# Moving the low-part subtractions of a split-precision attention and MoE kernel from GpSimd to VectorE

## Chip, cores and metric

The kernel runs on one core of a Trainium2 chip. The metric is the device time of one execution in microseconds (us). PE is TensorE, DVE is VectorE, ACT is ScalarE, POOL is GpSimd, SP is SyncE.

## Reference

```python
scores = scale * np.matmul(q, k.transpose(0, 1, 3, 2))   # 4 x 8 heads, 768 positions, 64 wide
keep = is_sink | in_window                               # 4 sink columns, a window of 128
a = softmax(np.where(keep, scores, -1e9))
x = np.matmul(a, v).transpose(0, 2, 1, 3).reshape(B * S, H * D)   # 3072 x 512
a = x @ w_a          # 512 x 1536
b = x @ w_b          # 512 x 1536
return (a * b @ w_out).astype(np.float32)                # 1536 x 512
```

The three weight matrices come as 64-bit floats; everything else is 32-bit.

## The kernel before

**Two halves.** A number that must be multiplied more exactly than one TensorE pass allows is kept as a high part (rounded to the type `F32R`) and a low part (the number less its high part). A product is then three matmuls: high by high, low by high, high by low. So every weight tile and every intermediate tile `g` (`a * b` of the MoE) needs a low part, which is one subtraction of 128x512 (`g` of the first chunk and all weights) or 128x384 and 128x256 (`g` of later chunks).

**Chunks.** The 3072 rows are worked through in 8 chunks (`CHUNKS`). The attention of chunk 0 (4 blocks of 128 rows) stands alone; then the MoE of chunk c (function `moe`) runs while the attention of chunk c + 1 is fed into it in small steps (`between`). The MoE goes over 12 values of j (`NJ`). For each j: `half("a", j)` (L686, 12 matmuls of up to 512 columns), ACT copies `a` out (L705), `half("b", j)` (L686), DVE multiplies the two into `g` (L711), ACT rounds `g` to `gh` (L714), one engine makes the low part `gl` (L716), and PE adds the product of the j before to the outputs (`project`, L695). `g` has one buffer, `gh` and `gl` two each.

**Attention of chunk 1.** It belongs to the MoE of chunk 0: a unit is a score matmul (L548) into the PSUM tile `s`, of which there is one; DVE reads it (L555), ACT takes the exponential (L557), DVE two small steps (L559, L560), ACT scales (L564), POOL copies 8 sink columns (L569), PE transposes (L585), ACT copies (L586), PE multiplies by v (L602), ACT copies the result (L604). So the next L548 waits until L555 has read the last one.

**Weights.** They are made once, 36 tiles of 128x512 in the order a, b, o of j = 0, 1, ..., from step 18 of the first attention on and throughout the MoE of chunk 0. The function `weights_to` sends each tile k through three stages, and a step does the low part of tile k - 4, the high part of tile k - 3 and the bits of tile k: `weight_low` (L317: subtraction), `weight_high` (L312: ACT rounds), `weight_bits` (L301 and L303 on DVE, L302 on ACT, L305 on POOL: the addition of the low words, 128x512). Before the change the low parts of the b tiles are made on POOL and those of the a and o tiles on DVE. `gl` is made on POOL for j below 10 and on DVE for j = 10 and 11, in every chunk.

**Order.** A scheduler puts each engine's instructions in order when the kernel is built; instructions passed through `keep_in_program_order` (`pin`) stay among themselves in the order in which they were written. Each engine runs its own list strictly in that order. By the order written, the low part of tile b of j + 1 stands behind L303 of tile b of j + 2 and in front of L301 of tile o of j + 2.

Of the kernel before, what the change touches and what calls it, by code (L numbers as in the profile page):

```python
# [7 lines left out]
F32 = mybir.dt.float32  # L8
# [5 lines left out]
ALU = mybir.AluOpType  # L14
# [3 lines left out]
B, H, S, D = 4, 8, 768, 64  # L18
DM, FF = 512, 1536
P = 128  # L20
# [3 lines left out]
NJ = FF // P  # L24
# [6 lines left out]
NEG = 8.0e9  # L31
BIG = 3.0e38
NIO = 6
POOL_LOW = (1, 3)
STEP0, STEPS = 18, 3
AHEAD, LOADS = 3, 9
D1, D2 = 3, 4
# [181 lines left out]
class Fast:  # L219
# [70 lines left out]
        self.nc.sync.dma_start(raw, self.src(kind)[j].bitcast(I32))  # L290
        self.raw[kind, j] = raw

    def low_engine(self, kind, j):
        return self.nc.gpsimd if (3 * j + "abo".index(kind)) % POOL_LOW[1] == POOL_LOW[0] else self.nc.vector

    def weight_bits(self, kind, j):
        nc, pin = self.nc, self.tc.keep_in_program_order
        rv = self.raw[kind, j].rearrange("p (n c) -> p n c", c=2)
        lo, hi = rv[:, :, 0], rv[:, :, 1]
        f = self.io([P, DM], I32, f"wf_{kind}{j}")  # L300
        pin(nc.vector.tensor_scalar(f, hi, 3, 0x3FFFFFF8, op0=ALU.logical_shift_left, op1=ALU.bitwise_and))  # L301
        pin(nc.scalar.activation(lo, lo.bitcast(U32), AF.Copy, scale=2.0 ** -29))  # L302
        nc.vector.scalar_tensor_tensor(out=f, in0=hi, scalar=I_TOP2, in1=f,  # L303
                                       op0=ALU.bitwise_and, op1=ALU.bitwise_or)
        nc.gpsimd.tensor_tensor(f, f, lo, op=ALU.add)  # L305
        del self.raw[kind, j]
        self.wf[kind, j] = f.bitcast(F32)
# [5 lines left out]

    def weight_low(self, kind, j):
        wh, wl = self.wt[kind, j]
        e = self.low_engine(kind, j)
        i = e.tensor_tensor(wl, self.wf.pop((kind, j)), wh.bitcast(F32), op=ALU.subtract)  # L317
        if e is self.nc.vector:
            self.tc.keep_in_program_order(i)

    def check_weight(self, kind, j):

# [346 lines left out]
            xs.append((xh, xl))  # L669
        return xs  # L670

    def moe(self, row, nt, xf, between, weights_ahead, last):
        nc = self.nc
        n = nt * P
        tag = f"{row}"
        xs = self.split_x(xf, nt, tag)
        outs = [self.ps.tile([P, DM], F32, tag=("o0", "o1", "o2", "av")[i], name=f"o{tag}_{i}") for i in range(nt)]

        def half(kind, j):
            wh, wl = self.wt[kind, j]  # L680
            ps = self.ps.tile([P, 4 * P], F32, tag=kind, name=f"{kind}{tag}_{j}")
            for kk in range(NK):
                ksl = slice(kk * P, (kk + 1) * P)
                xh, xl = xs[kk]
                for i, (w, x) in enumerate(((wh, xh), (wh, xl), (wl, xh))):
                    nc.tensor.matmul(ps[:, :n], lhsT=w[:, ksl], rhs=x[:, :n],  # L686
                                     start=kk == 0 and i == 0, stop=kk == NK - 1 and i == 2)
            return ps

        def project(j, gh, gl):  # L690
            wh, wl = self.wt["o", j]
            for i in range(nt):
                sl = slice(i * P, (i + 1) * P)
                for k, (g, w) in enumerate(((gh, wh), (gh, wl), (gl, wh))):
                    nc.tensor.matmul(outs[i], lhsT=g[:, sl], rhs=w,  # L695
                                     start=j == 0 and k == 0, stop=j == NJ - 1 and k == 2)

        prev = None
        for j in range(NJ):
            if last and j == 2:  # L700
                self.ok = self.verdict(self.ps.tile([1, P], F32, tag="s", name="gp"))
            weights_ahead(3 * j)
            pa = half("a", j)
            g = self.mo.tile([P, max(n, 3 * P)], F32, tag="g", name=f"g{tag}_{j}", bufs=1)
            nc.scalar.copy(g[:, :n], pa[:, :n])  # L705
            between(3 * j)
            if last and j == NJ - 1:
                self.tc.mark_branch_hint_location("general", hint="LikelyTaken", engines=mybir.ALL_ENGINES)
            weights_ahead(3 * j + 1)
            pb = half("b", j)  # L710
            nc.vector.tensor_tensor(g[:, :n], pb[:, :n], g[:, :n], op=ALU.mult)  # L711
            gh = self.mo.tile([P, max(n, 3 * P)], F32R, tag="gh", name=f"gh{tag}_{j}")
            gl = self.mo.tile([P, max(n, 3 * P)], F32R, tag="gl", name=f"gl{tag}_{j}")
            nc.scalar.copy(gh[:, :n], g[:, :n])  # L714
            e = nc.vector if j >= NJ - 2 else nc.gpsimd
            e.tensor_tensor(gl[:, :n], g[:, :n], gh[:, :n].bitcast(F32), op=ALU.subtract)  # L716
            between(3 * j + 1)
            weights_ahead(3 * j + 2)
            if prev is not None:
                project(*prev)  # L720
            between(3 * j + 2)
            prev = (j, gh, gl)
        project(*prev)
        for i in range(nt):
            r = row + i * P
            o = self.mo.tile([P, DM], F32, tag=("gh", "gl")[i % 2], name=f"os{tag}_{i}")
            (nc.vector.tensor_copy if last and i == 1 else nc.scalar.copy)(o, outs[i])
            (nc.sync if last else nc.scalar).dma_start(self.out[r:r + P, :], o)
# [4 lines left out]
    def run(self, scalars, verdict):  # L733
        chunks = CHUNKS
        order = [(k, j) for j in range(NJ) for k in "abo"]
        done, loaded = [0], [0]

        def weights_to(n, ahead):
            while loaded[0] < min(n + ahead, len(order)):
                self.load_weight(*order[loaded[0]])  # L740
                loaded[0] += 1
            while done[0] < min(n + D2, len(order) + D2):
                k = done[0]
                for d, stage in ((D2, self.weight_low), (D1, self.weight_high), (0, self.weight_bits)):
                    if 0 <= k - d < len(order):
                        stage(*order[k - d])
                done[0] += 1

        b, t0, nt = chunks[0]

        pairs = [self.wp.tile([P, 2, nt * P], F32, tag=f"w_{k}{NJ - 1}", name=f"xf0_{k}") for k in "bo"]
        xf = [x[:, i, :] for x in pairs for i in range(2)]
        first = self.attention(b, t0, nt, xf, exact=True, alone=True)
        next(first)
        val = scalars()
        self.masks(val)
        self.verdict = lambda gp: verdict(val, gp)
        for k, _ in enumerate(first, 1):
            if k >= STEP0 and (k - STEP0) % STEPS == 0:
                weights_to(done[0] + 1 - D2, 4 + D2)  # L760
        for c, (b, t0, nt) in enumerate(chunks):
            gen = None
            if c + 1 < len(chunks):
                nb, nt0, nnt = chunks[c + 1]
                nxf = self.new_xf(c + 1)
                gen = self.attention(nb, nt0, nnt, nxf, exact=c == 0)
                steps = H * nnt + (6 if c else 5)
            taken = [0]

            def between(s):  # L770
                if gen is None:
                    return
                want = min(steps, -(-steps * (s + 1) // (3 * NJ - 3)))
                while taken[0] < want:
                    next(gen, None)
                    taken[0] += 1

            def ahead(s):
                j = s // 3
                weights_to(max(s + AHEAD, done[0] + 1 - D2), LOADS)  # L780
                if s % 3:
                    return
                k = (c - 2) * 8 + j - 2
                if c >= 2 and 2 <= j < 10 and k < len(order):
                    self.check_weight(*order[k])
                elif self.unchecked:
                    self.check_weight(None, 0)

            self.moe(b * S + t0 * P, nt, xf, between, ahead, c + 1 == len(chunks))
            if gen is not None:  # L790
                for _ in gen:
                    pass
                xf = nxf
        return val, self.ok
# [73 lines left out]
```

## Time and profile before

| what | us |
|---|---|
| median of 3 runs | 810.65 (810.63 to 811.8) |
| the profiled execution | 809.97 |
| its span in the trace | 808.1 |
| around the span | 1.9 |

The span holds the instructions of all engines. In the rows further down, a time such as 76.13 is us from the start of the span, the next number is how long the instruction or the stretch lasted, and what stands in brackets behind a row is how long the engine sat idle before it and what ended that. An output is written before its inputs (`w_b<-wf_b,w_b`). The first MoE lies between about 47 and 188 us of the span.

### The profile page before, as it was taken

The numbers are of one execution on the slowest core, as the hardware profiler recorded it, in microseconds if no ns is written. First come the engines' busy times: TensorE is split into PE (matmuls) and PEld (weight loads), VectorE is DVE, ScalarE is ACT, GpSimd is POOL, SyncE is SP. The second block draws the span as 40 slices with busy tenths as digits, with TensorE's granted clock in tenths as the row PEclk, the third lists the DMA queues.
The fourth block names the chain that finished last, engine by engine and source line by source line (L and its number), as shares of the span: only waits on it lengthen the run. The fifth ranks groups of instructions, "written<-read, shape, count | busy, mean of one in ns | idle before, by whom it ended". The sixth has DMA issues, their size and how long they took to land.

```text
span 808.1 us, 13597 instructions
## 1 busy us (share of the span) xinstructions
PE 787.8 (97%) x4457; PEld 697.4 (86%) x4457; DVE 433.8 (54%) x1427; ACT 477.1 (59%) x1384; POOL 381.0 (47%) x483
## 2 busy tenths in 40 slices
PE   8997999999999999999999999999999999999997
PEld 5655777778989999999999999999999999999996
DVE  6889877834663555445654455535554456430101
ACT  5775665636774766567774677647674678631111
POOL 1248665673772564626653466515646266301110
PEclk9999999999999999999999999999999999999999
DMA  8866430031221133413323133231334132001001
GB/s 311 299 219 256 172 103 21 11 95 63 67 67 63 46 108 115 119 59 103 102 89 102 65 107 105 93 105 48 108 115 124 54 105 61 1 2 39 1 1 41
DMA packets 44778, 76.11 MB, mean 94 GB/s; under 512 B 4640, under 2 KB 24224, under 8 KB 44704
## 3 DMA queue, kind: packets, MB, share of 16 engines
q1 hardware_dynamic: 41648, 69.70, 26.9%
q10 hardware_dynamic: 3024, 5.51, 1.8%
q8 instruction: 36, 0.59, 0.3%
q14 instruction: 38, 0.31, 0.1%
q0 software_dynamic: 32, 0.00, 0.0%
HBM read 68.90 MB, written 6.29 MB: 93 GB/s over the span
## 4 chain that ended last, share of the span: by engine, by line
PE 87%; DVE 8%; ACT 2%; issue 1%; POOL 0%; DVEq 0%; ACTq 0%; POOLq 0%
PE o L695 23%; PE a L686 23%; PE b L686 23%; PE t L451 4%; PE s L419 4%; PE av L467 3%; PE s L548 2%; PE av L602 1%; PE t L585 1%; PE t L602 1%; DVE wf_a L303 1%; DVE wf_a L301 1%; DVE p L562 1%; DVE g L711 1%; PE sk L492 1%
## 5 line engine op out<-in xcount | busy, mean ns | idle before, releaser
L686 PE MATMUL a<-xh,w_a 128*128 128x384 f32 (+2 forms) x768 | 218.9, 345 | 0.0
L686 PE MATMUL b<-xh,w_b 128*128 128x384 f32 (+2 forms) x768 | 215.2, 343 | 0.0
L695 PE MATMUL o<-w_o,gh 128*128 128x512 f32 x576 | 186.8, 404 | 0.0
L716 POOL TENSOR_TENSOR gl<-g,gh 128x384 fp32r<-128x384 f32 (+2 forms) x80 | 83.2, 1040 | 197.9 <-ACT gh L714 195.0
L686 PEld LDWEIGHTS a<-xh,w_a 128*128 128x128 f32 x768 | 138.7, 188 | 6.5 <-issue 1.5
L686 PEld LDWEIGHTS b<-xh,w_b 128*128 128x128 f32 x768 | 138.8, 188 | 4.5 <-issue 0.8
L711 DVE TENSOR_TENSOR g<-b,g 128x384 f32<-128x384 f32 (+2 forms) x96 | 53.4, 556 | 150.6 <-PE b L686 142.8
L686 PE MATMUL a<-xl,w_a 128*128 128x384 f32 (+2 forms) x384 | 129.2, 337 | 0.9 <-DVE xl L668 0.9
L686 PE MATMUL b<-xl,w_b 128*128 128x384 f32 (+2 forms) x384 | 129.0, 336 | 0.0
L695 PEld LDWEIGHTS o<-w_o,gh 128*128 128x128 f32 x576 | 104.0, 188 | 19.5 <-issue 1.0
L695 PE MATMUL o<-w_o,gl 128*128 128x512 f32 x288 | 113.7, 396 | 0.6 <-POOL gl L716 0.6
L714 ACT CAST gh<-g 128x384 fp32r<-128x384 f32 (+2 forms) x96 | 49.4, 514 | 79.7 <-DVE g L711 77.7
L705 ACT COPY g<-a 128x384 f32<-128x384 f32 (+2 forms) x96 | 45.1, 470 | 79.5 <-PE a L686 69.9
L430 ACT ACTIVATE p<-p,st 128x128 f32<-128x128 f32 (+1 forms) x144 | 71.4, 496 | 26.3 <-DVE st L429 25.4
L426 ACT ACTIVATE p<-p,st 128x128 f32<-128x128 f32 (+1 forms) x144 | 71.6, 497 | 8.4 <-DVE st L424 8.3
L686 PEld LDWEIGHTS a<-xl,w_a 128*128 128x128 f32 x384 | 72.4, 189 | 3.5 <-DVE xl L668 1.3
L686 PEld LDWEIGHTS b<-xl,w_b 128*128 128x128 f32 x384 | 72.4, 188 | 2.0 <-issue 0.3
L454 ACT CAST pt<-t 128x128 fp32r<-128x128 f32 (+1 forms) x144 | 50.4, 350 | 39.1 <-PE t L451 37.3
L455 DVE TENSOR_TENSOR pt<-t,pt 128x128 fp32r<-128x128 f32 (+1 forms) x144 | 57.1, 397 | 20.9 <-ACT pt L454 19.4
L695 PEld LDWEIGHTS o<-w_o,gl 128*128 128x128 f32 x288 | 54.1, 188 | 14.2 <-POOL gl L716 1.0
L345 POOL TENSOR_SCALAR qh<-qr 128x384 fp32r<-128x384 f32 x48 | 24.6, 512 | 75.3 <-PE s L419 43.8
L424 DVE CUSTOM_DVE_ANT_0 p<-s,mg 128x264 f32<-128x264 f32 x96 | 41.1, 428 | 34.7 <-PE s L419 34.4
(141 smaller groups left out, 1334.7 us busy)
## 6 DMA issues: line engine op xcount, KB each, us to landing
qr<-in_qT_dram SPq DMA_DIRECT2D x48, 192.0 KB, 2.6
raw_a<-in_wa_dram SPq DMA_DIRECT2D x12, 512.0 KB, 6.4
raw_b<-in_wb_dram SPq DMA_DIRECT2D x12, 512.0 KB, 5.7
raw_o<-in_wo_dram SPq DMA_DIRECT2D x12, 512.0 KB, 6.2
chk_a<-in_wa_dram SPq DMA_DIRECT2D x24, 256.0 KB, 2.7
chk_b<-in_wb_dram SPq DMA_DIRECT2D x24, 256.0 KB, 2.7
chk_o<-in_wo_dram SPq DMA_DIRECT2D x24, 256.0 KB, 2.7
out_dram<-os ACTq DMA_DIRECT2D x21, 256.0 KB, 2.1
```

Source lines behind the costliest of these rows:

```text
L419: nc.tensor.matmul(ps[:, :w], lhsT=q[:, i * P:(i + 1) * P], rhs=ks[:, c0:c0 + w], start=m == 0, stop=m == 1)
L424: nc.vector.tensor_tensor_reduce(out=p[:, :w], in0=ps[:, :w], in1=m, scale=-0.125, scalar=BIG, op0=ALU.add, op1=ALU.min, accum_out=st[:, 0:1])
L426: nc.scalar.activation(p[:, :w], p[:, :w], AF.Exp, bias=st[:, 0:1], scale=-1.0, accum_out=st[:, 1:2])
L430: nc.scalar.mul(p[:, :w], p[:, :w], st[:, 3:4])
L454: nc.scalar.copy(hs, tp[:, :n, :])
L455: nc.vector.tensor_tensor(ls, tp[:, :n, :], hs.bitcast(F32), op=ALU.subtract)
L686: nc.tensor.matmul(ps[:, :n], lhsT=w[:, ksl], rhs=x[:, :n], start=kk == 0 and i == 0, stop=kk == NK - 1 and i == 2)
L695: nc.tensor.matmul(outs[i], lhsT=g[:, sl], rhs=w, start=j == 0 and k == 0, stop=j == NJ - 1 and k == 2)
L705: nc.scalar.copy(g[:, :n], pa[:, :n])
L711: nc.vector.tensor_tensor(g[:, :n], pb[:, :n], g[:, :n], op=ALU.mult)
L714: nc.scalar.copy(gh[:, :n], g[:, :n])
L716: e.tensor_tensor(gl[:, :n], g[:, :n], gh[:, :n].bitcast(F32), op=ALU.subtract)
```

## The change

All low parts of the weights are made on VectorE and are pinned in order there. In the MoE of chunk 0 `gl` is made on VectorE for every j; in the later chunks it stays as it was.

```diff
-POOL_LOW = (1, 3)
...
-    def low_engine(self, kind, j):
-        return self.nc.gpsimd if (3 * j + "abo".index(kind)) % POOL_LOW[1] == POOL_LOW[0] else self.nc.vector
-
...
     def weight_low(self, kind, j):
         wh, wl = self.wt[kind, j]
-        e = self.low_engine(kind, j)
-        i = e.tensor_tensor(wl, self.wf.pop((kind, j)), wh.bitcast(F32), op=ALU.subtract)
-        if e is self.nc.vector:
-            self.tc.keep_in_program_order(i)
+        self.tc.keep_in_program_order(
+            self.nc.vector.tensor_tensor(wl, self.wf.pop((kind, j)), wh.bitcast(F32), op=ALU.subtract))
...
-    def moe(self, row, nt, xf, between, weights_ahead, last):
+    def moe(self, row, nt, xf, between, weights_ahead, last, weights_split):
...
-            e = nc.vector if j >= NJ - 2 else nc.gpsimd
+            e = nc.gpsimd if weights_split and j < NJ - 2 else nc.vector
             e.tensor_tensor(gl[:, :n], g[:, :n], gh[:, :n].bitcast(F32), op=ALU.subtract)
...
-            self.moe(b * S + t0 * P, nt, xf, between, ahead, c + 1 == len(chunks))
+            self.moe(b * S + t0 * P, nt, xf, between, ahead, c + 1 == len(chunks), c > 0)
```

## Rows read from the trace of the kernel before

**Rows 1.** The page: busy time by engine, and the chain that ended last.
```profile
PE 787.8 (97%) x4457; PEld 697.4 (86%) x4457; DVE 433.8 (54%) x1427; ACT 477.1 (59%) x1384; POOL 381.0 (47%) x483
PE 87%; DVE 8%; ACT 2%; issue 1%; POOL 0%; DVEq 0%; ACTq 0%; POOLq 0%
```

**Rows 2.** Waits of PE, whole span: us in total, times, longest.
```profile
PE s L548 <- DVE st L555: 5.9, 3, 5.3
...
PE t L585 <- ACT xf L604: 1.3, 2, 0.7
```

**Rows 3.** Timeline of PE: around its longest wait, and a short one later.
```profile
76.13 0.40 PE L686 MATMUL b<-xh,w_b 128*128 128x512 f32 x1
81.78 1.25 PE L548 MATMUL s<-kx,qx 128*128 128x264 f32 x2 [5.25 <-DVE st L555]
...
112.23 0.44 PE L585 MATMUL t<-ident,p 128*128 128x128 f32 x2 [0.66 <-ACT xf L604]
```

**Rows 4.** Stretches of 2 us: busy PE, PEld, DVE, ACT, POOL; PEclk, DMA, GB/s.
```profile
80.00:82.00 2.00, 0.22 (x1) 0.22 (x2) 1.73 (x3) 0.24 (x1) 1.31 (x2) 0.87 1.03 400
82.00:84.00 2.00, 2.00 (x7) 1.32 (x8) 1.53 (x5) 1.73 (x5) 0.99 (x2) 0.50 0.95 385
84.00:86.00 2.00, 2.00 (x10) 1.33 (x9) 1.12 (x6) 1.61 (x5) 1.70 (x2) 0.78 0.08 33
```

**Rows 5.** Timeline of DVE ahead of the end of that wait.
```profile
59.26 1.77 DVE L317 TENSOR_TENSOR w_a<-wf_a,w_a 128x512 fp32r<-128x512 f32 x1
...
62.58 0.68 DVE L711 TENSOR_TENSOR g<-b,g 128x512 f32<-128x512 f32 x1
63.18 1.21 DVE L303 SCALAR_TENSOR_TENSOR wf_o<-raw_o,wf_o 128x512 int32<-128x512 int32 x1
...
72.76 0.68 DVE L711 TENSOR_TENSOR g<-b,g 128x512 f32<-128x512 f32 x1
...
73.61 0.93 DVE L317 TENSOR_TENSOR w_o<-wf_o,w_o 128x512 fp32r<-128x512 f32 x1
...
76.04 1.65 DVE L303 SCALAR_TENSOR_TENSOR wf_a<-raw_a,wf_a 128x512 int32<-128x512 int32 x1
...
78.21 1.48 DVE L301 TENSOR_SCALAR wf_b<-raw_b 128x512 int32<-128x512 int32 x1
...
81.30 0.42 DVE L555 CUSTOM_DVE_ANT_0 p<-s,mg 128x264 f32<-128x264 f32 x1
```

**Rows 6.** Timeline of POOL in the same stretch, and once later.
```profile
75.67 1.46 POOL L716 TENSOR_TENSOR gl<-g,gh 128x512 fp32r<-128x512 f32 x1
...
77.70 1.71 POOL L317 TENSOR_TENSOR w_b<-wf_b,w_b 128x512 fp32r<-128x512 f32 x1
...
108.19 1.74 POOL L716 TENSOR_TENSOR gl<-g,gh 128x512 fp32r<-128x512 f32 x1
```

**Rows 7.** One line each: duration ns min/median/max, first and last start.
```profile
L301 DVE TENSOR_SCALAR wf_b<-raw_b x12: 396/415/1539, 32.3 to 157.6; 128x512 int32<-128x512 int32 x12
L303 DVE SCALAR_TENSOR_TENSOR wf_a<-raw_a,wf_a x12: 675/692/1647, 29.2 to 156.4; 128x512 int32<-128x512 int32 x12
L317 DVE TENSOR_TENSOR w_a<-wf_a,w_a x12: 669/682/1783, 47.8 to 169.3; 128x512 fp32r<-128x512 f32 x12
L305 POOL TENSOR_TENSOR wf_a<-wf_a,raw_a x12: 1285/1302/1762, 30.0 to 157.7; 128x512 int32<-128x512 int32 x12
```

**Rows 8.** Stretches: the late DVE queue, and one j afterwards (columns as above).
```profile
57.40:81.70 24.30, 17.62 (x75) 13.21 (x73) 24.13 (x29) 13.00 (x26) 20.54 (x16) 1.00 0.72 268
...
112.00:124.00 12.00, 11.77 (x57) 9.22 (x57) 8.06 (x19) 7.78 (x18) 7.59 (x8) 1.00 0.07 19
```

**Rows 9.** Timeline of DVE: behind a `gl` on POOL, and `gl` on DVE.
```profile
108.71 1.49 DVE L301 TENSOR_SCALAR wf_a<-raw_a 128x512 int32<-128x512 int32 x1
...
184.43 0.69 DVE L716 TENSOR_TENSOR gl<-g,gh 128x512 fp32r<-128x512 f32 x1 [0.36 <-ACT gh L714]
```

**Rows 10.** Waits of all engines, 40 to 190 us.
```profile
POOL w_b L317 <- ACT w_b L312: 7.4, 6, 2.1
```

## Prediction

> **What bounds the kernel now.** I began with the page. PE is busy for 97% of the span, and the chain that ended last is 87% PE and 8% DVE [rows 1]. So work on DVE and POOL matters only where PE waits for it, and the change touches only the weights and the first MoE. The second view was therefore the waits of PE. They are few, and two kinds of them lie in the first MoE: 5.9 us for the score matmul L548, nearly all of it one wait of 5.3, and 1.3 us in two waits for the transposes L585 [rows 2].
>
> The third view was the timeline around the long wait. PE finishes `b` of j = 2 at about 76.5 us and starts again at 81.78, after 5.25 us of idling, released by L555 [rows 3]. L555 starts at 81.30 [rows 5]. The score it reads was ready long before; it was late because DVE's list was late. From 57.4 to 81.7 us DVE is busy for 24.13 of 24.30 us with only 29 instructions [rows 8]: this stretch, and not PE, sets the time here. The granted clock shows a second cost of the wait. It is at 0.50, the 1.2 GHz level, from 82 to 84 us (2.4 GHz is 1.00), and at 0.87 and 0.78 in the two stretches beside it [rows 4].
>
> The fourth view says why DVE is so slow there. Undisturbed, L301, L303 and L317 take about 0.41, 0.68 and 0.68 us [rows 7]. In the late stretch many take 1.5 to 1.8 us [rows 5], and each of those begins while a POOL instruction is under way: L303 at 76.04 lasts 1.65 us beside POOL's `gl` of 75.67, and L301 at 78.21 lasts 1.48 beside w_b of 77.70 [rows 5, 6]; w_a at 59.26 lasts 1.77 beside an earlier w_b. The DVE instruction ends 0.3 to 0.6 us after POOL's (L303 at 77.69, `gl` at 77.13), so it did its own work only when POOL had finished. L711, which reads PSUM, stays at 0.68 us [rows 5]. So a POOL subtraction costs DVE about 1 us when a DVE instruction on SBUF stands behind it, and nothing otherwise.
>
> **Part 1: the long wait.** Ahead of L555 at 81.30, five POOL instructions go: three low parts w_b and two `gl`, of which the last of each kind stand in [rows 6]. Their holds on DVE are the durations less the undisturbed ones: 1.77 - 0.68 = 1.09 for the first w_b, the same for the second, 1.48 - 0.41 = 1.07 for the third, and 1.65 - 0.68 = 0.97 for each `gl` [rows 5, 7]. Together 5.2 us. Added to DVE ahead of L555 are two `gl` and two w_b; the third w_b is written behind the L303 that stands just before L555, in front of L301 of tile o, and so comes after it. Four instructions of 0.68 us [rows 7, 9] are 2.7 us. Net gain 2.5 us.
>
> Not all of it will stay. The additions of the low words, L305, remain on POOL, at 1.3 us each [rows 7]. Two of them now hold DVE for little, because L711 or another short instruction ran meanwhile: L303 at 63.18 was held for 1.21 - 0.68 = 0.53 us and L317 at 73.61 for 0.93 - 0.68 = 0.25 [rows 5]. With one more SBUF instruction on DVE beside each, both may hold for the full 1.1, which takes back 0.57 + 0.85 = 1.4. Also, a POOL with less to do starts its additions sooner, and one more could come ahead of L555, another 1.1. So the gain here lies between nothing (2.5 - 1.4 - 1.1) and 2.5 us; more than the 5.25 of the wait is excluded. I take 1.8, above the middle, by the check that follows.
>
> As a check, one j of the late stretch takes 72.76 - 62.58 = 10.2 us from L711 to L711 [rows 5]. Afterwards it needs three tiles of 0.41 + 0.68 + 0.68 on DVE, 5.3 us, plus L711 and `gl` at 0.68 each, 1.4, plus at most three holds of 1.1, 3.3: 10.0 at worst, and less where an addition lies under L711 or L555. Two j then gain 0.4 us at worst and 2.6 if one hold in each is hidden. That brackets the 1.8.
>
> The rule that speaks against this change is in the Trainium skill, page "Perfetto Trace Analysis", section "Optimizing Scalar/DVE Operations": GpSimd and DVE share an SBUF port, so moving work between those two might not help. By it this part would bring nothing; by the rows each exchange is a hold of about 1.05 us against 0.68 of DVE's own work. The trace agrees that the two engines stand in each other's way, and not that the exchange is even.
>
> **Part 2: the clock.** The mean of 0.87 from 80 to 82 us is full speed for 74% of it and half for the rest, so the fall came at about 81.5, some 5 us after PE went idle; the mean of 0.78 from 84 to 86 is half speed for 44% of it, so it was back at full at about 84.9 [rows 4]. PE ran from 81.78 to 84.9 at half speed and lost half of 3.1 us, 1.55. If PE resumes at 81.78 - 1.8 = 80.0, before the moment at which the clock fell, I expect no fall and book the whole 1.55. The bounds are 0 and 1.55.
>
> **Part 3: the two waits of 0.66.** The first ends at 112.23 us and the second comes two j later [rows 3]; PE waits there for an ACT copy (L604) that stands behind an exponential, which waits for a late L555. One of the instructions ahead of that L555 is L301 at 108.71, 1.49 us instead of 0.41, held by the `gl` of 108.19 on POOL [rows 6, 9]. The hold of 1.08 is replaced by 0.68 on DVE, a gain of 0.4 in each: 0.8. Against it, a `gl` or w_b may now stand in front of an L555 elsewhere. Bounds 1.3 gain and 1.3 loss; I take 0.6 gain.
>
> **What costs nothing.** The remaining seven or so w_b and eight `gl` on DVE are covered, since per j DVE is busy for about 8.1 of 12 us after the late stretch [rows 8] and 2 x 0.68 fits; without that cover they would cost 1.4 us per j. `gl` on DVE waits for ACT's `gh`: at 184.43 that wait is 0.36 us [rows 9]. Behind it are queued the next low part, L301 and L555, and PE's next score waits for L555. No DMA is issued or moved. Later chunks keep their code and begin earlier by the same amount, since PE is what they wait for.
>
> **Sum.** 1.8 + 1.55 + 0.6 = 3.95 us. The profiled execution took 809.97 us (span 808.1 and 1.9 around it), so 806.0. The median of the runs is 0.7 above the profiled one; I put the forecast at 806.4.
>
> **Rivals.** *No change.* Each removed hold is replaced by DVE's own 0.68 us and by fuller holds of L305; PE resumes within 0.3 us of 81.78 and the clock still falls. The time is 809.0 to 812. For it: the lower bound of part 1. Against it: five holds go and only four instructions, each shorter than a hold, come ahead of L555. It is what the rule of the Trainium skill's page "Perfetto Trace Analysis" named above comes to as a mechanism.
>
> *The wait shortens, but the clock falls all the same,* because PE still idles for 3.5 us. Then 1.8 + 0.6 is left, 808.2 to 809.6.
>
> *Slower: the in-order list of DVE takes on POOL's waits.* POOL waited six times, 7.4 us in all, for ACT's rounding before a w_b [rows 10]. POOL had little else to do then; on DVE, the same wait would stop L301, L711 and L555 behind it, and with L555 the single score tile. If each of the seven heads of chunk 1 still to come finds a w_b or `gl` of 0.68 us in front of its L555, PE pays 4.8 us: about 815. It decides once DVE's time per j passes PE's, which is some 11.8 us of the 12 shown [rows 8]. Against it: 10.0 at worst for tiles, L711 and `gl`, plus L555 and small steps of about 1; close, but under. The written order also puts w_b behind L303 of a later tile, where ACT has had more time.
>
> *Larger gain.* The long wait goes almost wholly: 5.25 + 1.55 + 0.6 is 7.4, about 803.
>
> **How the numbers follow.** Forecast 0.54, with its own range of 803.5 to 808.3; clock falls all the same 0.13; no change 0.15; slower 0.13; larger gain 0.05. About 0.2%, or 1.6 us, is what a measurement of this kernel can tell from no change. The second case is split evenly by that bound (below 809.0 or not), so faster is 0.54 + 0.05 + 0.07 = 0.66, same 0.15 + 0.06 = 0.21, slower 0.13. The range of 802.5 to 811 leaves out the slower case and the edges of the others.
>
> **What would show it.** Right: the longest wait of PE falls from 5.3 us to about 3.5 and ends near 80; the granted clock is 1.00 throughout; DVE's L301, L303 and L317 in the late stretch reach 1.5 us or more beside L305 alone; one j there takes 9 to 9.8 us. Wrong: L555 is still at 81 or later; the clock is at 0.50 again; PE gathers waits of 0.5 us or more between 88 and 175 us behind L555 or `gl`. The prediction fails above all if the scheduler orders DVE's list differently around L555 once it has these extra instructions, because the long wait comes from what stands in front of that one instruction.

## The result and the profile after

The changed kernel takes 805.75 us (median, 805.63 to 806.1) against 810.64 of the kernel before on the same chip (809.97 to 811.8): a ratio of 0.9935 with an interval of 0.9922 to 0.9949, so 0.65% faster. The forecast was 806.4. The profiled execution took 806.1 us with a span of 804.2, which is 3.9 us less than the profiled one of before. The medians differ by 4.9: before, the profiled execution lay 0.7 under its median, and after 0.35 above it. What follows explains the 3.9 that the two traces show.

The changed lines stand a few numbers lower in the code of after: L301, L303, L305 and L317 are now L297, L299, L301 and L313; L548 and L555 are L542 and L549; L604 is L598; L686 and L695 are L680 and L689; L711, L714 and L716 are L705, L708 and L710.

The page after, busy time by engine and the chain that ended last, answering to [rows 1]:

```profile
PE 787.0 (98%) x4457; PEld 697.5 (87%) x4457; DVE 431.7 (54%) x1449; ACT 477.2 (59%) x1384; POOL 351.4 (44%) x461
PE 88%; DVE 7%; ACT 2%; issue 1%; DMA 1%; DVEq 0%; ACTq 0%; POOLq 0%
```

22 instructions have gone from POOL to DVE (12 low parts w_b and 10 `gl`). POOL is busy for 29.6 us less, and DVE, with 22 instructions more, for 2.1 us *less*: 22 of 0.68 us were added, 15 us, and more than that went out of the instructions that DVE already had.

The waits of PE in the whole span (us in total, times, longest), answering to [rows 2]:

```profile
PE s L542 <- DVE st L549: 4.3, 3, 2.9
...
PE b L680 <- DVE g L705: 1.3, 1, 1.3
```

The long wait is 2.9 us and no longer 5.3. The two waits of the transposes for ACT's L598 have left the list. One wait is new, for DVE's `g`, at 64.42 us. In its place two waits of before are gone that the prediction did not count: 0.92 us at 59.39 for DVE's `xl` and 0.59 us at 67.64 for POOL's `gl`. The first `a` of j = 2 starts at 70.07 us before and at 70.09 after, so up to there nothing is won or lost.

PE's timeline at the long wait, answering to [rows 3]:

```profile
76.05 0.40 PE L680 MATMUL b<-xh,w_b 128*128 128x512 f32 x1
79.30 0.71 PE L542 MATMUL s<-kx,qx 128*128 128x264 f32 x2 [2.86 <-DVE st L549]
79.95 1.89 PE L596 MATMUL t<-ptx,vx 128*64 128x128 f32 x8
```

The stretches, answering to [rows 4, 8] (busy PE, PEld, DVE, ACT, POOL; PEclk, DMA, GB/s):

```profile
57.40:81.70 24.30, 20.17 (x86) 15.00 (x84) 24.16 (x40) 15.93 (x32) 14.64 (x12) 0.97 0.77 284
...
80.00:82.00 2.00, 2.00 (x10) 1.67 (x10) 1.97 (x4) 0.51 (x1) 1.82 (x2) 0.52 1.02 401
82.00:84.00 2.00, 2.00 (x7) 1.25 (x8) 2.00 (x6) 1.20 (x3) 0.56 (x1) 0.63 0.52 213
84.00:86.00 2.00, 2.00 (x11) 1.63 (x10) 1.97 (x4) 1.43 (x5) 0.75 (x1) 1.00 0.03 10
...
112.00:124.00 12.00, 12.00 (x58) 8.89 (x57) 8.38 (x23) 7.93 (x19) 4.58 (x6) 1.00 0.12 33
```

Two things are to be read here. In the late stretch DVE is as full as before, but gets 40 instructions done where it got 29. And the clock fell nevertheless: 0.52 and 0.63 say that it was at the 1.2 GHz level from about 80.1 us (4% of the first stretch at full) to about 83.5 (74% of the second at half). PE had been running again for 0.8 us when it fell, and lost half of 3.4 us, 1.7 us.

DVE's timeline ahead of that wait's end, answering to [rows 5], and POOL's, answering to [rows 6]:

```profile
73.21 1.00 DVE L313 TENSOR_TENSOR w_o<-wf_o,w_o 128x512 fp32r<-128x512 f32 x1
74.13 1.54 DVE L297 TENSOR_SCALAR wf_a<-raw_a 128x512 int32<-128x512 int32 x1
75.59 0.68 DVE L710 TENSOR_TENSOR gl<-g,gh 128x512 fp32r<-128x512 f32 x1
76.19 0.68 DVE L299 SCALAR_TENSOR_TENSOR wf_a<-raw_a,wf_a 128x512 int32<-128x512 int32 x1
76.79 0.68 DVE L313 TENSOR_TENSOR w_a<-wf_a,w_a 128x512 fp32r<-128x512 f32 x1
77.39 1.50 DVE L297 TENSOR_SCALAR wf_b<-raw_b 128x512 int32<-128x512 int32 x1
78.82 0.42 DVE L549 CUSTOM_DVE_ANT_0 p<-s,mg 128x264 f32<-128x264 f32 x1
79.17 0.68 DVE L299 SCALAR_TENSOR_TENSOR wf_b<-raw_b,wf_b 128x512 int32<-128x512 int32 x1
```

```profile
73.61 1.77 POOL L301 TENSOR_TENSOR wf_o<-wf_o,raw_o 128x512 int32<-128x512 int32 x1
...
77.00 1.61 POOL L301 TENSOR_TENSOR wf_a<-wf_a,raw_a 128x512 int32<-128x512 int32 x1 [0.68 <-POOL sc L563]
```

Each DVE instruction that is still long (1.54 at 74.13, 1.50 at 77.39) lies beside one of POOL's additions of the low words and ends 0.3 us after it; between the two additions DVE's instructions start every 0.60 us. The time by which an instruction lasts longer than the undisturbed ones of [rows 7] is called a hold here. From 57.4 us to the score's reader there are 12 holds of 11.4 us in sum before (reader at 81.30), and 7 of 7.0 us after (reader at 78.82), all seven beside L301 of POOL. Note the order of the last two rows of DVE: L549 now stands *in front of* L299 of tile b, where before it stood behind it.

The Trainium skill, page "SBUF — State Buffer", section "Who interferes with whom", says that a DVE instruction with two SBUF inputs contends with a GpSimd instruction that reads SBUF and that one with at most one SBUF input outside certain modes does not, and that where the shared port pair is taken the second to issue blocks for the whole of the other's instruction. The trace agrees: L297 (one input, of an operation that the page counts among those with such modes), L299 and L313 (two inputs) wait out POOL's instruction, while L705 and L549, which take one input from PSUM, keep to 0.68 and 0.42 us in both kernels.

Landmarks of PE in the first MoE, before and then after: its first `a`, the first `a` of j = 3, and an `a` behind each of the two short waits of before. Before:

```profile
47.45 0.50 PE L686 MATMUL a<-xh,w_a 128*128 128x512 f32 x1
...
88.02 0.40 PE L686 MATMUL a<-xh,w_a 128*128 128x512 f32 x1
...
112.42 0.48 PE L686 MATMUL a<-xh,w_a 128*128 128x512 f32 x1
...
136.23 0.48 PE L686 MATMUL a<-xh,w_a 128*128 128x512 f32 x1
```

After:

```profile
47.48 0.59 PE L680 MATMUL a<-xh,w_a 128*128 128x512 f32 x1
...
85.83 0.39 PE L680 MATMUL a<-xh,w_a 128*128 128x512 f32 x1
...
109.33 0.47 PE L680 MATMUL a<-xh,w_a 128*128 128x512 f32 x1
...
132.25 0.47 PE L680 MATMUL a<-xh,w_a 128*128 128x512 f32 x1
```

The gain grows from 2.2 to 3.1 to 4.0 us, and stays there to the end of the span. Of the 2.2, the wait that ends at 79.30 and not 81.78 gave 2.5, and 0.3 was lost behind it: half of that is the clock (1.7 us lost and not 1.55), the other half no row shows. Each short wait gave 0.9: its 0.66, and 0.24 that no single row shows.

### The profile page after: what moved, and what is told of

Read it like the earlier page. It is cut to its first block, busy times and chain, and to the rows that moved or that the text cites. A ratio compares the mean times of both kernels' runs of the same rounds, so it can differ in the third digit from the quotient of the medians.

```text
span 804.2 us, 13606 instructions
## 1 busy us (share of the span) xinstructions
PE 787.0 (98%) x4457; PEld 697.5 (87%) x4457; DVE 431.7 (54%) x1449; ACT 477.2 (59%) x1384; POOL 351.4 (44%) x461
## 4 chain that ended last, share of the span: by engine, by line
PE 88%; DVE 7%; ACT 2%; issue 1%; DMA 1%; DVEq 0%; ACTq 0%; POOLq 0%
PE o L689 24%; PE a L680 23%; PE b L680 23%; PE t L445 4%; PE s L413 4%; PE av L461 3%; PE s L542 2%; PE av L596 1%; PE t L596 1%; PE t L579 1%; DVE p L556 1%; ACT p L420 1%; DVE g L705 1%; PE sk L486 1%; DVE wf_b L297 0%
## 5 line engine op out<-in xcount | busy, mean ns | idle before, releaser
L680 PE MATMUL a<-xh,w_a 128*128 128x384 f32 (+2 forms) x768 | 218.8, 345 | 0.0
L680 PE MATMUL b<-xh,w_b 128*128 128x384 f32 (+2 forms) x768 | 215.6, 343 | 1.3 <-DVE g L705 1.3
L689 PE MATMUL o<-w_o,gh 128*128 128x512 f32 x576 | 187.3, 405 | 0.0
L710 POOL TENSOR_TENSOR gl<-g,gh 128x384 fp32r<-128x384 f32 (+1 forms) x70 | 68.3, 976 | 197.4 <-ACT gh L708 194.5
L680 PEld LDWEIGHTS b<-xh,w_b 128*128 128x128 f32 x768 | 138.8, 188 | 6.5 <-DVE g L705 1.7
L680 PEld LDWEIGHTS a<-xh,w_a 128*128 128x128 f32 x768 | 138.7, 188 | 6.4 <-issue 1.5
L705 DVE TENSOR_TENSOR g<-b,g 128x384 f32<-128x384 f32 (+2 forms) x96 | 53.4, 557 | 148.0 <-PE b L680 135.4
L680 PE MATMUL a<-xl,w_a 128*128 128x384 f32 (+2 forms) x384 | 129.2, 336 | 0.0
L680 PE MATMUL b<-xl,w_b 128*128 128x384 f32 (+2 forms) x384 | 128.9, 336 | 0.0
L689 PEld LDWEIGHTS o<-w_o,gh 128*128 128x128 f32 x576 | 104.4, 189 | 19.6 <-issue 1.0
L689 PE MATMUL o<-w_o,gl 128*128 128x512 f32 x288 | 113.8, 396 | 0.0
L708 ACT CAST gh<-g 128x384 fp32r<-128x384 f32 (+2 forms) x96 | 49.4, 514 | 83.0 <-DVE g L705 81.1
L680 PEld LDWEIGHTS a<-xl,w_a 128*128 128x128 f32 x384 | 72.4, 189 | 2.6 <-DVE xl L662 0.4
L680 PEld LDWEIGHTS b<-xl,w_b 128*128 128x128 f32 x384 | 72.4, 188 | 1.6
L689 PEld LDWEIGHTS o<-w_o,gl 128*128 128x128 f32 x288 | 54.2, 188 | 13.2 <-DVE gl L710 0.8
L342 POOL TENSOR_TENSOR ks<-kr,ks 64x400 fp32r<-64x400 f32 (+1 forms) x48 | 57.6, 1200 | 3.9
```

The source lines that it names most:

```text
L342: self.nc.gpsimd.tensor_tensor(o, i, high.bitcast(F32), op=ALU.subtract)
L680: nc.tensor.matmul(ps[:, :n], lhsT=w[:, ksl], rhs=x[:, :n], start=kk == 0 and i == 0, stop=kk == NK - 1 and i == 2)
L689: nc.tensor.matmul(outs[i], lhsT=g[:, sl], rhs=w, start=j == 0 and k == 0, stop=j == NJ - 1 and k == 2)
```

## Experiments

Each ratio is to the kernel before on the same chip: 811.04 us for experiments 1 to 4, 811.10 for 5 to 8, 810.91 for 9 and 10. A trace is one execution, and in those of 1, 9 and 10 the first MoE starts 1 to 2 us later than in the others, after 3.4 us at the 1.2 GHz level in the first attention. So places in the first MoE are compared by their distance from its first `a`.

| experiment | us | ratio to before, interval |
|---|---|---|
| the change itself | 805.75 | 0.9935, 0.9922 to 0.9949 |
| 1 w_b alone | 809.35 | 0.9981, 0.9967 to 0.9995 |
| 2 `gl` alone | 807.96 | 0.9961, 0.9948 to 0.9974 |
| 3 the 22 on neither engine | 803.42 | 0.9906, 0.9892 to 0.9921 |
| 4 the change, L549 put back | 806.50 | 0.9942, 0.9929 to 0.9955 |
| 5 the 22 on both engines | 816.70 | 1.0071, 1.0055 to 1.0087 |
| 6 the change, additions on DVE too | 799.70 | 0.9862, 0.9842 to 0.9881 |
| 7 the change, `project` first | 808.63 | 0.9974, 0.9961 to 0.9987 |
| 8 before, `project` first | 815.97 | 1.0049, 1.0032 to 1.0066 |
| 9 before, additions on DVE | 807.95 | 0.9959, 0.9944 to 0.9974 |
| 10 as 6 | 800.96 | 0.9874, 0.9856 to 0.9892 |

**1 and 2: one part alone.** Against the changed kernel, experiment 1 leaves `gl` on POOL:

```diff
-            e = nc.gpsimd if weights_split and j < NJ - 2 else nc.vector
+            e = nc.gpsimd if j < NJ - 2 else nc.vector
```

> Only the low parts of the b weights move to VectorE; gl stays on GpSimd as before. Theory (each GpSimd subtraction holds VectorE for about 1.05 us, its replacement costs 0.6 us of VectorE's list): ahead of the long wait three holds go (3.3 us) and two subtractions come (1.2), less some 0.6 of holds that grow, so the wait of 5.25 us shortens by about 1.5; the two short waits of 0.66 us stay, since gl on GpSimd still holds VectorE there; the clock still falls. About 809.1 us (808.4 to 809.9). Rival (the gain is the scheduler's other order of VectorE's list, in which the score's reader L549 comes one instruction earlier; exchanges as such are even): here that order is the one of before, so within 0.4 us of 810.6.

Experiment 2 is the kernel before with `gl` of the first MoE on DVE and w_b left on POOL:

```diff
...
-            e = nc.vector if j >= NJ - 2 else nc.gpsimd
+            e = nc.gpsimd if weights_split and j < NJ - 2 else nc.vector
...
```

> Only gl of the first MoE moves to VectorE; the low parts of the b weights stay on GpSimd. Theory: ahead of the long wait two holds go (1.9 us) and two subtractions come (1.2), so it shortens by about 0.7; both short waits at 112 and 136 us vanish, worth 0.9 each by the starts of the matmuls behind them in the two traces (1.8 together). About 808.1 us (807.4 to 809.0). Rival (order alone): the score's reader stands where it stood before, so 810.2 to 811.

Measured: 809.35 and 807.96 us, gains of 1.7 and 3.1 within the ranges expected, which add up to about the 4.9 of both. PE's timeline at the first `a`, at the long wait and at the first of the short ones, of experiment 1:

```profile
48.95 0.59 PE L680 MATMUL a<-xh,w_a 128*128 128x512 f32 x1
...
82.42 0.89 PE L542 MATMUL s<-kx,qx 128*128 128x264 f32 x2 [3.94 <-DVE st L549]
...
112.48 0.44 PE L579 MATMUL t<-ident,p 128*128 128x128 f32 x2 [0.16 <-ACT xf L598]
```

Counted from the first `a`, the long wait ends at 33.5 us and not at 34.3 as before: with w_b alone the wait is 1.3 us shorter, where about 1.5 was expected, but PE comes to it 0.4 us later and resumes only 0.9 us sooner. The two short waits were expected to stay, yet they shrink from 0.66 to 0.16 us, although the `gl` to which I had put the first of them is still on POOL. So the time came out in the range, but in part by other terms than expected. With `gl` alone the short waits go wholly, and the long wait ends 0.7 us sooner (33.6 us from the first `a`), both as expected. The two times add up, then, but their parts don't: the short waits are won largely by either move, and the long wait ends 2.5 us sooner with both moves where the two alone make 1.6. Experiment 4 shows where most of the rest comes from. In experiment 2 the clock also stays low for longer:

```profile
80.00:82.00 2.00, 0.92 (x2) 0.50 (x2) 1.29 (x6) 0.94 (x3) 1.19 (x1) 0.57 1.02 399
...
86.00:88.00 2.00, 2.00 (x9) 1.70 (x8) 1.36 (x3) 1.30 (x3) 0.30 (x1) 0.72 0.00 0
```

By these means it fell at 80.3 and came back at 87.1 us, twice the 3.4 us of after. This profiled execution took 808.78, the longest of its five; its mean granted clock is 0.994 and that of each of the other four 0.997, so they spent less time at the lower level.

**3: the 22 on neither engine.** In the changed kernel the low parts of the b tiles, and `gl` of the first MoE for j below 10, are not made; the high part is used in their place, and all matmuls remain.

```diff
+        f = self.wf.pop((kind, j))
+        if kind == "b":
+            self.wt[kind, j] = (wh, wh)
+            return
...
+            if not weights_split and j < NJ - 2:
+                gl = gh
...
```

> As the changed kernel, but the low parts of the b weights and gl of the first MoE for j below 10 are not made at all; the matmuls take the high part in their place, so PE's work is the same. Theory: the holds are gone and VectorE's own four subtractions ahead of the long wait (2.4 us) too; the wait of 2.9 us shrinks to 0.5 to 1, and then the clock should not fall (1.7 us): 801.5 to 802.5 us; 803.3 if the clock falls all the same. Rival (VectorE's own subtractions cost nothing, only the order or GpSimd's relief counts): 805.4 to 806.

Measured: 803.42 us. PE's timeline:

```profile
77.01 0.71 PE L546 MATMUL s<-kx,qx 128*128 128x264 f32 x2 [1.19 <-DVE st L553]
...
81.11 0.44 PE L583 MATMUL t<-ident,p 128*128 128x128 f32 x2 [1.23 <-ACT xf L602]
```

The clock stayed at 1.00 in this execution, so the 1.7 us are back; but two waits of 1.2 us remain, with only the additions and the sink copies left on POOL. I had expected 1 us less. What DVE's 22 instructions cost in the changed kernel is 805.75 - 803.42 = 2.3 us. By the profiled executions 1.7 of that is the clock, and in experiment 3 the scheduler put the score's reader behind L299 again, so the order is in this difference too.

**5: the 22 on both engines.** DVE's list is that of the changed kernel; POOL repeats each moved subtraction into the same tile.

```diff
+        if kind == "b":
+            self.nc.gpsimd.tensor_tensor(wl, f, wh.bitcast(F32), op=ALU.subtract)
...
+            if not weights_split and j < NJ - 2:
+                nc.gpsimd.tensor_tensor(gl[:, :n], g[:, :n], gh[:, :n].bitcast(F32), op=ALU.subtract)
```

> The changed kernel, in which GpSimd repeats each moved subtraction (low parts of the b weights, gl of the first MoE for j below 10) into the same tile after VectorE has made it. VectorE's list is instruction for instruction that of the changed kernel; only GpSimd's work is back. Theory (holds): four to five more holds of 1.05 us ahead of the long wait, so it grows from 2.9 to 7 or 8 us, and short waits come back (0 to 1.8): 810.0 to 812.8 us, no faster than before. Rival (order of VectorE's list decides and holds do not): 805.4 to 806.4. Rival (holds matter only half, since GpSimd waits as often as VectorE): about 808.

Measured: 816.70 us, 4 us beyond what I expected. PE's waits, and a window over the rest of the first MoE:

```profile
PE s L545 <- DVE st L552: 4.6, 2, 4.2
PE t L582 <- DVE sct L612: 3.9, 3, 1.6
...
PE o L692 <- POOL gl L715: 1.3, 1, 1.3
```

```profile
88.00:160.00 72.00, 67.92 (x313) 51.10 (x311) 64.81 (x114) 42.67 (x96) 46.46 (x42) 0.99 0.20 65
```

DVE's list is the same, instruction for instruction, and the reader comes 3.7 us later than in the changed kernel, counted from the first `a`. That is what the holds beside the repeated instructions ahead of it come to: 0.5 and three of 1.1 us. The long wait still grew to 4.2 us only, not to 7 or 8, because PE itself came later; 1.3 us of that is its wait for POOL's second `gl`, a price of the repeat that is no hold. PE is idle for 4.1 us between 88 and 160, where DVE is now 90% busy: this is the slower rival's in-order list of DVE, brought about by holds, since DVE's waits for ACT there are no longer than in the changed kernel. Together with experiment 3 there are four corners:

| us | POOL makes the 22 not | POOL makes them |
|---|---|---|
| DVE makes the 22 not | 803.42 (3) | 811.0 (before) |
| DVE makes them | 805.75 (after) | 816.70 (5) |

The same 22 subtractions cost 7.6 us on POOL and 2.3 on DVE; where the other engine makes them too, 10.95 and 5.7. The clock is in these numbers: in the profiled executions it fell in the first MoE of all but experiment 3, which is 1.55 us of the 7.6 and 1.7 of the 2.3. So the exchange is not even, and what those on POOL cost shows in DVE's durations: holds of 11.4 us ahead of the reader before against 7.0 after. The rule of the Trainium skill named in the prediction (page "Perfetto Trace Analysis") holds in that the two engines stand in each other's way; that moving work between them might not help does not hold for this direction, in which the instruction leaves the engine that holds the other.

**4: the order alone.** Two pins put L549 back behind L299 of tile b of j = 4 in the changed kernel:

```diff
+        if (kind, j) == ("b", 4):
+            pin(i)
...
+            if not alone and (h, i) == (1, 1):
+                self.tc.keep_in_program_order(r)
```

> The changed kernel with one thing forced: the score's reader L549 that ends the long wait stands behind L299 of the same b tile again, as in the kernel before, instead of one place ahead of it. Theory: the wait grows by L299's own 0.6 us, or by 1.1 where an addition on GpSimd gets in between; 806.4 to 807.4 us, so that at least two thirds of the 4.9 us stay. Rival (order alone): back to 809 or more.

Measured: 806.50 us. PE's timeline:

```profile
80.24 1.03 PE L544 MATMUL s<-kx,qx 128*128 128x264 f32 x2 [3.56 <-DVE st L551]
```

The wait is 0.70 us longer than after's 2.86, and the time 0.75 longer. The two ratios' intervals overlap, so the time by itself would not settle it, but the row does: of the gain about 0.7 us comes from the scheduler's order, which was not part of the edit.

**6 and 10: the additions too.** If holds are the cause, the additions that still hold DVE should be worth more than they cost there:

```diff
-        nc.gpsimd.tensor_tensor(f, f, lo, op=ALU.add)
+        nc.vector.tensor_tensor(f, f, lo, op=ALU.add)
```

> The changed kernel with the last GpSimd work on the weights moved too: the addition of the low words runs on VectorE (which adds these integers by way of floats, so the weights are rounded otherwise). Theory: some seven holds of 1.1 us ahead of the long wait become seven additions of 0.6, so the wait shrinks by 2 to 2.9 and nearly goes, and with less than 2 us of idling the clock stays up (1.7): 801.5 to 803.5 us. Rival (VectorE becomes the bound, since it now also takes on GpSimd's waits for ACT's conversion of the low words): 807 or more.

> The fastest kernel so far once more, in more rounds beside the kernel before: 799.2 to 800.5 us.

Measured: 799.70 and, on another occasion, 800.96 us: 1.3 to 1.4% faster than before and 0.6 to 0.7% faster than the change. That is better than the 801.5 to 803.5 that I gave first, and the second is just above its range. The late stretch, and two groups by line with minimum, median and maximum in ns, of experiment 6:

```profile
57.40:81.70 24.30, 23.70 (x108) 18.51 (x107) 22.69 (x51) 18.11 (x40) 5.69 (x4) 1.00 0.89 329
```

```profile
L313 DVE TENSOR_TENSOR w_a<-wf_a,w_a x12: 669/682/697, 46.8 to 158.9; 128x512 fp32r<-128x512 f32 x12
...
L301 DVE CUSTOM_DVE_ANT_0 wf_a<-raw_a,wf_a x12: 669/683/696, 30.0 to 147.5; 128x1024 uint16<-128x1024 uint16 x12
```

No instruction of L313 is held any more: its maximum is 0.70 us where it was 1.81. DVE does 51 instructions in the stretch in which it did 40, and has 1.6 us to spare; PE never waits for long, and the clock stays at 1.00. The gain against after in the first MoE is 2.86 (the wait) + 1.7 (the clock) + 1.27 (the wait for `g` at 64.42) = 5.8, which leaves out three short waits that experiment 6 has there (0.95 us in sum) and so is not the whole account. It was 5.9 and 6.0, from the first `a` of the MoE to its first output copy: 182.47 - 47.48 = 135.0 us after, 175.89 - 46.84 = 129.0 in 6 and 177.50 - 48.49 = 129.0 in 10. The two profiled executions differ by 1.92 us, and 1.65 of that lies ahead of the MoE. There the clock was at the 1.2 GHz level from 44.3 to 47.7 us in 10, and not in 6:

```profile
44.00:46.00 2.00, 1.95 (x9) 1.42 (x9) 1.80 (x8) 1.96 (x6) 0.19 (x1) 0.58 0.94 350
46.00:48.00 2.00, 2.00 (x8) 1.33 (x9) 1.03 (x7) 0.71 (x3) 0.00 (x0) 0.57 0.95 250
```

**9: the additions alone.** The same edit in the kernel before:

```diff
-        nc.gpsimd.tensor_tensor(f, f, lo, op=ALU.add)
+        nc.vector.tensor_tensor(f, f, lo, op=ALU.add)
```

> The kernel before, with only the addition of the low words moved from GpSimd to VectorE; the low parts of the b weights and gl of the first MoE stay on GpSimd. Theory (every hold counts alike, whichever instruction makes it): per j two GpSimd instructions are left instead of five before and three in the changed kernel, for three more on VectorE of 0.6 us; ahead of the long wait seven holds of 1.05 go and seven additions come, a gain of some 3 us, 1 us more in the first attention, where the additions held its scaling, and 1.7 if the clock then stays up: 804 to 806.5 us. Rival (the additions cost nothing, since the gain of 6 us by moving them last came only because no GpSimd instruction was left): 809 or more.

Measured: 807.95 us, between the two theories. The long wait is down to 0.86 us, but others have grown or are new, and the cause of the longest stands above it in the timeline, on POOL and DVE:

```profile
60.35 1.29 POOL L317 TENSOR_TENSOR w_b<-wf_b,w_b 128x512 fp32r<-128x512 f32 x1 [7.91 <-ACT w_b L312]
...
60.44 1.76 DVE L668 TENSOR_TENSOR xl<-xf_o,xh 128x512 fp32r<-128x512 f32 x1
...
62.26 0.50 PE L686 MATMUL a<-xl,w_a 128*128 128x512 f32 x1 [1.71 <-DVE xl L668]
...
99.19 0.44 PE L585 MATMUL t<-ident,p 128*128 128x128 f32 x2 [1.64 <-DVE sct L615]
```

A w_b that starts 0.09 us ahead of DVE's `xl` holds it for 1.1 us, and PE's next matmul waits for `xl`. In the kernel before an addition holds the same `xl` for as long, and PE waits 0.92 us. The waits for `sct` (the transposed sink columns, which DVE copies out of PSUM), 1.64 us here and 0.96 at 123.18, are not there before. From the first `a` to the first output copy this trace is 2.8 us shorter than before; 1.55 of that is the clock, which did not fall in this stretch, so the waits are only about 1.2 us less. So the 36 additions moved here bring less than the 22 subtractions, although each holds as long. What a hold costs is what the held instruction holds up, not the hold's length.

**7 and 8: more work for PE ahead of the score.** PE's own list has the score matmul ahead of `project`, whose inputs come from the j before. Here `project` is put first, in the changed kernel (7) and, for the first MoE likewise, in the kernel before (8):

```diff
-            between(3 * j + 1)
+            if weights_split:
+                between(3 * j + 1)
             weights_ahead(3 * j + 2)
             if prev is not None:
                 project(*prev)
+            if not weights_split:
+                between(3 * j + 1)
```

> The changed kernel, in which the first MoE writes the product of the j before ahead of the attention steps of that place, so that PE has 2.8 us of matmuls to do where it now waits 2.9 us. Nothing of VectorE's or GpSimd's work is taken away. Theory (the wait and the clock are what is left to win here): the wait goes, the clock does not fall, 801.0 to 802.5 us. Rival (the attention steps, made later, bring new waits at the transposes): 804 to 806.5.

> The kernel before with the same reordering of PE's work, and with its GpSimd work as it was. Theory (the change won by shortening one wait of PE): 2.8 of the 5.25 us are filled, and some 2.4 are left, so about 808.0 us, or 806.5 if the clock stays up; the short waits remain. So most of the change's gain is had without moving a single subtraction. Rival (holds slow VectorE wherever it is needed, and the wait is only where it shows): 809.5 or more.

Measured: 808.63 and 815.97 us, both far from what I expected; 8 is 0.5% slower than before. PE's longest wait in 7:

```profile
87.84 0.69 PE L579 MATMUL t<-ident,p 128*128 128x128 f32 x2 [5.78 <-ACT xf L598]
```

and what DVE did ahead of that wait's end in 7:

```profile
75.39 0.69 DVE L710 TENSOR_TENSOR gl<-g,gh 128x512 fp32r<-128x512 f32 x1 [3.34 <-ACT gh L708]
...
82.46 0.68 DVE L705 TENSOR_TENSOR g<-b,g 128x512 f32<-128x512 f32 x1
83.06 0.67 DVE L299 SCALAR_TENSOR_TENSOR wf_o<-raw_o,wf_o 128x512 int32<-128x512 int32 x1
83.82 0.69 DVE L710 TENSOR_TENSOR gl<-g,gh 128x512 fp32r<-128x512 f32 x1
84.43 1.78 DVE L313 TENSOR_TENSOR w_o<-wf_o,w_o 128x512 fp32r<-128x512 f32 x1
86.13 0.41 DVE L297 TENSOR_SCALAR wf_a<-raw_a 128x512 int32<-128x512 int32 x1
86.47 0.42 DVE L549 CUSTOM_DVE_ANT_0 p<-s,mg 128x264 f32<-128x264 f32 x1
```

My theory was that PE idled for want of something to do. It falls: the wait that stood at the score is gone, but one twice as long stands at a transpose behind it. PE waits there for an ACT copy behind an exponential, and that waits for the late reader L549 at 86.47. The edit is not one of PE's order alone, though. The attention steps of that place are now written behind the weight work for every engine, and in 7 this reader stands behind `gl`, w_o and L297 of tile a, which come after it in the changed kernel (reader at 83.22, `gl` at 83.58). DVE also stood idle for 3.34 us at 75.39, waiting for ACT's `gh`. In 8 `project` itself waits once 2.26 us for POOL's `gl`. So these two runs show that this reordering loses, and that DVE's list is late here; that no order of PE's list alone would help, they don't show.

## Why the prediction was right, and where it was not

The time (806.4 forecast, 805.75 measured) and the direction were right, the time in part by luck. Of the three terms one was wrong in sign, and two were too small by about as much: 1.8 + 1.55 + 0.6 = 3.95 us was forecast, 2.5 - 0.3 + 1.8 = 4.0 is what the traces show, and the errors of +0.7, -1.85 and +1.2 cancel. One of the prediction's own signs of being wrong, a clock at 0.50 again, came true.

- **Part 1, the long wait: right mechanism, size 1.8 forecast, 2.5 measured**, at the upper bound. Holds fell by 4.4 us in sum: the five that go are worth 5.2, as costed, and only 0.8 of the 1.4 came back as fuller holds of the additions. The four instructions added cost 0.60 each from start to start, 2.4 and not 2.7. And L549 was put ahead of L299, 0.6 to 0.7 us, which the prediction named as its point of failure; it went the other way. The check of one j was too cautious: 8.7 us from `g` (63.69) to `g` (72.36) where 9 to 9.8 was the sign. The sign that what is still held stands beside L305 (now L301) alone came true: all seven holds do, and six of the instructions reach 1.5 us or more.
- **Part 2, the clock: +1.55 forecast, -0.3 measured** (-0.15 by the granted clock, and as much behind the wait that no row shows). The step that failed is "before the moment at which the clock fell, I expect no fall". It took the moment of one trace, 5.0 us after PE went idle, for a fixed one. After, it fell 3.6 us after the idle began and 0.8 after PE had resumed. The rival that named this (wait shorter, clock falls all the same) was right on the clock and wrong on the time, because it took the other two terms as forecast.
- **Part 3, the short waits: +0.6 forecast, 1.8 measured.** Both are gone, and each was worth 0.9. That moving `gl` ends them is right (experiment 2), but the step that names L301 at 108.71, held by the `gl` of 108.19, is too narrow: experiment 1 keeps that `gl` on POOL, and only 0.16 us of each wait is left. Which hold of the several in such a j decides was not isolated. No L549 came late in their place: PE is busy for 12.00 of the 12 us from 112 to 124.
- **What costs nothing** held: between 112 and 124 DVE is busy for 8.4 of 12 us, with 4 instructions more than before.
- **No change** is refuted by the time and by the four corners (2.3 us against 7.6). **Slower** did not happen; experiment 5 shows that its mechanism is real once DVE carries the instructions and the holds as well. **Larger gain** needed the long wait to vanish, which experiment 6 did by moving the additions too.

## What to carry to other kernels

Where two engines hold each other up, cost an instruction by what it does to the other engine's list at that place: here 22 subtractions cost 7.6 us on POOL and 2.3 on DVE, though DVE was the late engine. A stretch that is bound by one engine's in-order list was shortened here by taking time out of that list; the one attempt to give the waiting engine something else to do first made it longer, and it moved the late engine's list as well. And a forecast should not bank a clock recovery from an idle time that only gets shorter: here it stayed away. Where PE's waits went almost wholly (experiments 6 and 10) the clock held in the first MoE, though in 10 it fell ahead of it.

## What the runs showed of the hardware

- The clock's fall does not follow the idle time closely. In the first MoE PE's idles of 2.86 us (after), 3.56 (4), 3.94 (1), 4.20 (5), 4.92 (2), 5.25 (before) and 5.78 (7) all came with a fall to the 1.2 GHz level, the first 0.8 us after PE had resumed; idles of 1.19 and 1.23 (3) and of 1.71 (9) did not, but one of 1.07 (8) did, so the 2 us of idling in the expectation of experiment 6 is no bound. The low lasted 3.4 us before and after, and 6.8 us in experiments 2, 5 and 7.
- The same work can meet a fall in one execution and not in another. In experiment 1 the clock fell at 45.28 us, in the first attention, behind waits of PE of 0.35, 0.50 and 0.42 us; in the changed kernel the same three waits (0.35, 0.50 and 0.43) stand at the same times within 0.02 us, and the clock stayed at 1.00. What decides is not shown.
- An addition of 128x512 int32 runs on DVE as one custom instruction over 128x1024 16-bit halves in 0.68 us, half of POOL's 1.3. Its duration was the same in all 12 instructions of the group (0.669 to 0.696). Whether it rounds as the expectation of experiment 6 says, no run here shows.
- A hold of DVE reaches the short instruction as well: L297 has one wide input and a constant and takes 0.41 us alone, but 1.5 beside POOL's addition.
